# Packed attention into a softplus FFN: scores issued beside the products of M, one run for both groups' packed values, and written queues for VectorE and ScalarE

## The chip, the cores and the metric

The kernel runs on one core of a Trainium2 chip. The metric is the device time in microseconds of one execution; three executions are known. A profile of one execution gives the engines' rows.

## What is computed

```python
q, k, v: (8, 8, 576, 64)   p: (8, 8, 32, 64)   w_in: (512, 2048)   w_out: (2048, 512)   float32
packed = softmax(scale * p @ k.T) @ v          # 32 packed values per head
att    = softmax(scale * q @ packed.T) @ packed
x      = att, heads side by side               # (8 * 576, 512)
h      = x @ w_in
out    = (max(h, 0) + log1p(exp(-abs(h)))) @ w_out
```

## The kernel before

A batch has 8 heads in G = 2 groups of 4 (HG). The second attention's product with the packed values is never made on its own: with M = packed @ w_in for each head, h is (attention weights) @ M, so that a batch needs M (`make_m`, float32, 64 rows by 32 columns of the array, 16 matmul records for each 512 columns of M) and then `gemm1`. Weights and M are split into a high and a low float32r part; each product is three matmuls.

The main loop runs over 128 **units**, one for each batch b and each of 16 column blocks f of the hidden layer. In a unit TensorE (PE) does, in this order: `gemm1` (L551: 12 matmuls of 288 columns, six for each half c of the 576 rows, into the two banks `ph` of the pool `ps_h`), then for t = 0 to 3 `gemm2_tile` of the unit two before (L594: three matmuls of 512 columns each), and every fourth unit (f = 2, 6, 10, 14) the products of M for two units on. The softplus of a half c is on ScalarE (ACT) `Abs` (L576), `Exp` (L577), `Ln` (L578) and on VectorE (DVE) the last step that reads the bank `ph` (L581, `SCALAR_TENSOR_TENSOR`, called STT here); then DVE makes `gh` (L566) and `gl` (L567), which PE needs two units later. The bank `ph` of a half is free when its STT is done.

The attention of batch b+1 is a generator of which the loop takes a step now and then, so that its work falls between the `gemm2_tile` calls of batch b: four visits to the scores on PE (`scores1` and `scores2`, L291, 16 records of 288 columns, 64 rows by 32 columns), two visits to the packed values (`packed`, L346, 48 records of 64 columns), transposes of the first softmax's weights (L336, copied by ACT at L337) and of the packed values (L359). DVE transposes k and q (L274), transposes the second scores out of PSUM (L370) and does most of the second softmax: `softmax2_exp` and `softmax2_div`, the second of which is a chain of five instructions that each need the one before (sum L387, add L388, reciprocal L389, product L390, transpose L394). Scores, packed values, transposes and M's products all take their PSUM banks from the two of the pool `ps_m`. At f = 15 `weights` splits the attention weights (ACT L307, DVE L495).

Every second batch `rests` adds the 64 rows that are over from two batches: at f = 1 of an even batch, behind the stores of the batch before, eight pieces of six matmuls each (L594, `acc_m`), for each of which DVE first makes `gh_m` and `gl_m` (L566, L567).

PE's queue is written down: it issues in the order of the program. The orders of DVE and ACT are chosen by the scheduler of the language.

Of the kernel before, what the change touches and what calls it, by code (L numbers as in the profile page):

```python
# [26 lines left out]
def pack_attention_then_softplus_ffn(  # L27
# [14 lines left out]
    P = 128  # L42
# [40 lines left out]

    spare = []

    def bank(nm):
# [16 lines left out]
    def pack_transposed(bg, t):  # L103
        for o in range(0, H, HG):
            ps = bank(f"ppt_{bg}_{o}")
            for i in range(HG):
                nc.tensor.transpose(ps[:D, i * P:(i + 1) * P], t[:, o + i, :], ident)
            dst = pT[:, o:o + HG, :].rearrange("x h j -> x (h j)")
            nc.vector.tensor_copy(dst[:D], ps[:D])
            nc.scalar.copy(dst[D:], ps[:D])  # L110
# [230 lines left out]
    def packed(b, g, a1T, rs):  # L341

        ps = bank(f"psp_{b}_{g}")
        for s in range(SI):
# [18 lines left out]

    def scores2(b, g, c, qT):
        pt = res[b]["pt"][g]
        ps = scores(2, b, g, c, lambda hh: pt[:, hh * J:(hh + 1) * J], qT)
        a2 = work.tile([P, C], F32, tag="a2", name=f"a2_{b}_{g}_{c}", bufs=3)
        nc.vector.transpose(a2, ps)  # L370
# [26 lines left out]
    def attention(b):  # L397
# [211 lines left out]
    def out_tile(nm):  # L609
        return cv.tile([P, 2, DM], F32, tag="x", name=f"o_{nm}", bufs=2)  # L610
# [75 lines left out]
    gs, acc = {}, None  # L686
    units = [(b, f) for b in range(B) for f in range(NF)]
    ahead, chain, due = iter(()), iter(()), 0.0
    for u in range(len(units) + LAG):
        if u < len(units):  # L690
            b, f = units[u]
            if f == 0:
                if (b + 1) % BG == 0 and b + 1 < B:
                    pack_transposed((b + 1) // BG, pt)
                ahead = attention(b + 1) if b + 1 < B else iter(())
                due = 0.0
            chain = softplus(b, f, gemm1(b, f, res[b]), gs)
            next(chain)
            if f == NF - 1:
                if (b + 2) % BG == 0 and b + 2 < B:  # L700
                    pt = load_pack((b + 2) // BG, (nc.sync,))
                for _ in ahead:
                    pass
                if b + 1 < B:
                    weights(b + 1)
        if u >= LAG:
            b2, f2 = units[u - LAG]
            gh, gl = gs.pop((b2, f2))
            if f2 == 0:
                acc = [ps_acc.tile([P, DM], F32, tag="acc", name=f"acc_{b2}_{t}") for t in range(NT)]  # L710
        last = u >= LAG and f2 == NF - 1 and b2 % 2 == 1
        if last:
            both = rests(b2)
            next(both)
        for t in range(NT):
            if u >= LAG:
                gemm2_tile(
                    acc[t], gh, gl, f2, slice(t * P, (t + 1) * P), f2 == 0, f2 == NF - 1
                )
                if f2 == NF - 1:  # L720
                    if t % 2 == 0:
                        o = out_tile(f"{b2}_{t}")
                    store(o[:, t % 2], acc[t], [(0, b2, t * P, P)])
# [48 lines left out]
```

## Time and profile before

| | us |
|---|---|
| executions | 775.4, 775.71, 776.82 |
| median | 775.71 |
| the profiled execution | 775.68 |
| its span, first to last instruction | 773.5 |
| PE busy | 745.7 (96%) |
| DVE busy | 535.8 (69%) |
| ACT busy | 436.5 (56%) |
| mean granted clock of PE | 0.986 of 2.4 GHz |

About 2.2 us lie outside the span. In the rows below a time is from the start of the span, "us" is the duration of the instruction, and `x16` is a count of rows merged into one. Matmuls overlap in the pipeline, so that what one costs is the distance between two starts, not its duration.

### The profile page before, as it was taken

To read this page: it belongs to the slowest core of one execution; us is meant where nothing else is said; L and a number is where in the kernel's file an instruction comes from. 1 tells how busy PE (TensorE), PEld (TensorE's weight loads), DVE (VectorE), ACT (ScalarE), POOL (GpSimd) and SP (SyncE) were. 2 spreads that over 40 slices of the span, in tenths; PEclk is the share of its full clock that TensorE was granted. 3 is DMA by queue.
4 is the path that set the end of the run, shared out by engine and by line. 5 is a ranking of instruction groups with operands and counts; after the bars stand their busy time and mean duration, and the time that the engine had idled before them with its cause. 6 is when DMAs were issued, how large, how long until landed. Compare 5 with 4: busy or idle time off the path is not lost.

```text
span 773.5 us, 14441 instructions
## 1 busy us (share of the span) xinstructions
PE 745.7 (96%) x5436; PEld 589.6 (76%) x5436; DVE 535.8 (69%) x1264; ACT 436.5 (56%) x1086; POOL 92.3 (12%) x166
## 2 busy tenths in 40 slices
PE   6888998899999999999999999999999999999997
PEld 4766776677788787777788777877887777888886
DVE  2688799975787557875687567875687557765553
ACT  5668787556454555665554455565554465565540
POOL 1415443200000000000000000000000000000110
PEclk9789999999999999999999999999999999999999
DMA  9976655652322334124122233225122200010001
GB/s 229 242 166 174 171 157 138 102 107 42 62 39 70 53 62 75 32 73 76 31 48 70 45 62 59 35 66 83 32 39 78 45 1 2 0 55 1 1 1 68
DMA packets 163397, 55.97 MB, mean 72 GB/s; under 512 B 143872, under 2 KB 156672, under 8 KB 163328
## 3 DMA queue, kind: packets, MB, share of 16 engines
q1 hardware_dynamic: 162704, 54.80, 32.7%
q8 instruction: 42, 0.69, 0.4%
q10 hardware_dynamic: 624, 0.26, 0.1%
q14 instruction: 27, 0.22, 0.1%
HBM read 45.61 MB, written 9.44 MB: 71 GB/s over the span
## 4 chain that ended last, share of the span: by engine, by line
PE 84%; DVE 7%; ACT 3%; DMA 3%; issue 1%; SPq 1%; POOL 0%; DVEq 0%; ACTq 0%; POOLq 0%
PE acc L594 43%; PE ph L551 26%; PE acc_m L594 6%; PE psm L513 4%; PE ps L291 3%; PE psp L346 2%; DMA q<-in_q 2%; PE psa L336 1%; DVE t L218 1%; DMA x_i<-in_moe_w_in 1%; DVE t L213 1%; ACT m L207 1%; DVE wo_l L253 1%; DVE e L581 1%; PE psT_q L278 1%
## 5 line engine op out<-in xcount | busy, mean ns | idle before, releaser
L576 ACT ACTIVATE e<-ph 128x288 f32<-128x288 f32 x256 | 102.8, 403 | 208.5 <-PE ph L551 191.3
L581 DVE SCALAR_TENSOR_TENSOR e<-ph,e 128x288 f32<-128x288 f32 x256 | 113.8, 452 | 145.0 <-ACT e L578 144.9
L594 PE MATMUL acc<-wo_h,gh 128*128 128x512 f32 x512 | 208.0, 406 | 0.0
L594 PE MATMUL acc<-wo_l,gh 128*128 128x512 f32 x512 | 201.5, 393 | 0.0
L594 PE MATMUL acc<-wo_h,gl 128*128 128x512 f32 x512 | 201.3, 393 | 0.0
L551 PE MATMUL ph<-at_h,mh 128*128 128x288 f32 x512 | 157.7, 309 | 4.3 <-DVE e L581 4.1
L551 PE MATMUL ph<-at_l,mh 128*128 128x288 f32 x512 | 151.3, 298 | 1.3 <-DVE at_l L495 1.1
L551 PE MATMUL ph<-at_h,ml 128*128 128x288 f32 x512 | 151.6, 296 | 0.0
L551 PEld LDWEIGHTS ph<-at_h,mh 128*128 128x128 f32 x512 | 96.5, 189 | 39.8 <-DVE gl L567 16.8
L587 POOL COPY rest<-e 128x64 f32<-128x64 f32 x128 | 46.8, 366 | 581.5 <-DVE e L581 568.4
L594 PEld LDWEIGHTS acc<-wo_h,gh 128*128 128x128 f32 x512 | 96.5, 189 | 25.3 <-issue 9.8
L594 PEld LDWEIGHTS acc<-wo_h,gl 128*128 128x128 f32 x512 | 96.5, 189 | 21.5
L577 ACT ACTIVATE e<-e 128x288 f32<-128x288 f32 (+1 forms) x240 | 109.2, 455 | 3.6
L578 ACT ACTIVATE e<-e 128x288 f32<-128x288 f32 (+1 forms) x240 | 109.3, 455 | 2.9
L594 PEld LDWEIGHTS acc<-wo_l,gh 128*128 128x128 f32 x512 | 96.7, 189 | 13.2
L551 PEld LDWEIGHTS ph<-at_l,mh 128*128 128x128 f32 x512 | 96.4, 189 | 6.0 <-DVE at_l L495 3.4
L551 PEld LDWEIGHTS ph<-at_h,ml 128*128 128x128 f32 x512 | 96.7, 189 | 0.2
L567 DVE TENSOR_TENSOR gl<-e,gh 128x512 fp32r<-128x512 f32 x128 | 86.8, 678 | 4.9
L566 DVE CAST gh<-e 128x512 fp32r<-128x512 f32 x128 | 58.0, 453 | 5.6
L528 ACT CAST mh<-psm 128x512 fp32r<-128x512 f32 (+1 forms) x72 | 35.6, 543 | 40.8 <-PE psm L513 40.7
L529 DVE TENSOR_TENSOR ml<-psm,mh 128x512 fp32r<-128x512 f32 (+1 forms) x72 | 42.5, 621 | 16.9 <-ACT mh L528 16.9
L513 PE MATMUL psm<-w_in_sb,pt 64*32 64x512 f32 (+1 forms) x576 | 40.4, 561 | 4.6 <-ACT a1T L337 1.9
(79 smaller groups left out, 750.6 us busy)
## 6 DMA issues: line engine op xcount, KB each, us to landing
v<-in_v SPq DMA_DIRECT2D x16, 576.0 KB, 5.1
x_i<-in_moe_w_in SPq DMA_DIRECT2D x32, 256.0 KB, 4.8
x_o<-in_moe_w_out SPq DMA_DIRECT2D x16, 512.0 KB, 3.6
k<-in_k SPq DMA_DIRECT2D x48, 144.0 KB, 3.2
q<-in_q SPq DMA_DIRECT2D x48, 144.0 KB, 3.0
out<-o SPq DMA_DIRECT2D x24, 256.0 KB, 2.0
k<-in_k SPq DMA_DIRECT2D x4, 576.0 KB, 9.9
q<-in_q SPq DMA_DIRECT2D x4, 576.0 KB, 9.1
```

What stands on the lines that cost most here:

```text
L513: nc.tensor.matmul(ps[hh * J:(hh + 1) * J, :n], res["pt"][g][o:o + D, hh * J:(hh + 1) * J], w_in_sb[o:o + D, hh, c * n:(c + 1) * n], start ...
L528: nc.scalar.copy(mh[:, cols], ps[:, :n])
L529: nc.vector.tensor_tensor(ml[:, cols], ps[:, :n], mh[:, cols].bitcast(F32), op=ALU.subtract)
L551: nc.tensor.matmul(ph[:, :C], x[:, o:o + P], y[:, g, cs], start=(i == 0), stop=(i == 3 * G - 1),)
L566: nc.vector.tensor_copy(hi, x)
L567: nc.vector.tensor_tensor(lo, x, hi.bitcast(F32), op=ALU.subtract)
L576: nc.scalar.activation(es[c], hv[c], AF.Abs)
L577: nc.scalar.activation(e[:, x], e[:, x], AF.Exp, scale=-1.0)
L578: nc.scalar.activation(e[:, x], e[:, x], AF.Ln, bias=1.0)
L581: nc.vector.scalar_tensor_tensor(es[c], hv[c], 0.0, es[c], op0=ALU.max, op1=ALU.add)
L587: nc.gpsimd.tensor_copy(rest[:, rest_at(b, f), r:r + REST], e[:, NT * P:])
L594: nc.tensor.matmul(acc, x[:, cs], y[:, f, :], start=(first and i == 0), stop=(last and i == 2),)
```

## The change

Five edits:

- The attention of batches 2 to 7 is no longer a generator. `attention_in_slots(b)` fills a table `steps`: at unit (b-1)*16+f, slot t = 0 to 3 (behind the `gemm2_tile` of that t) or slot END = 4 (behind all four, just ahead of M's products) stands a list of calls. Batches 0 and 1 keep the generator.
- The four pairs of scores of a batch go to slot END of f = 14 (of the batch before), 2, 6 and 10, directly ahead of `make_m`, and take the two banks of `ps_h` instead of banks of `ps_m` (batch 2's first pair keeps `ps_m` and slot 0 of f = 2).
- The packed values of both groups are one run of 96 records into one bank (slot 0 of f = 5).
- From unit 16 on DVE and ACT issue in the order of the program too. For these units softplus is `Abs`, `Exp`, `Ln` of half 0, then of half 1, ahead of slot 0; the STT of half 0 is emitted behind the calls of slot 0, that of half 1 behind those of slot 2, `gh` and `gl` behind those of slot 3; stores come behind them.
- The buffers `a2` go from three to two, `pp` from one to two; the packing of p for batches 4 to 7 moves from the end of batch 2 into it.

```diff
+        def pair(nm, g):
+            return [bank(f"ps{nm}_{b}_{g}_{c}", ps_h) for c in range(2)]
...
+        def pack():
+            pp["ps"] = bank(f"psp_{b}")
+            for g in range(G):
+                pack_products(b, g, a1T[g], pp["ps"][:, g * D:])
...
+        END = NT
+        early = b == BY_BLOCK
+        for hh in range(HG):
+            if early:
+                at(hh // 2, hh % 2 * 2 + 1, move, "k", 0, hh)
+                at(2, hh, move, "k", 1, hh)
+            else:
+                at(hh // 2 - 3, hh % 2 * (1 + (hh < 2)) + (hh < 2), move, "k", 0, hh)
+                at(hh // 2 * 2, hh % 2 * (1 + (hh < 2)) + (hh < 2), move, "k", 1, hh)
+            at(3 + hh // 2, 1 + hh % 2 * 2, move, "q", 0, hh)
+            at(9 + hh // 2, hh % 2 * (1 + (hh < 2)) + (hh < 2), move, "q", 1, hh)
+        if early:
+            steps[(b - 1) * NF + 2, 0].insert(0, (score1, (0, False)))
+            n = 2
+        else:
+            at(-2, END, score1, 0)
+            n = 0
...
+        at(n, 2, exp1, 0)
...
+        at(n, 0, turn1, 0, 0)
+        at(n, 2, turn1, 0, 1)
+        at(2, END, score1, 1)
+        at(2, END, load, "q", b, 1)
+        at(4, 0, max1, 1)
+        at(4, 0, exp1, 1)
+        at(5, 0, sum1, 1)
+        at(4, END, turn1, 1, 0)
+        at(4, END, turn1, 1, 1)
+        at(5, 0, pack)
+        for g in range(G):
+            at(5, 0, load, "k", b + 1, g)
+            at(5, 1, scale_pack, g)
+            at(5, 3, turn_pack, g)
+        for g in range(G):
+            f = 6 + 4 * g
+            at(f, END, score2, g)
+            at(f, END, load, "v", b + 1, g)
+            for c in range(2):
+                at(f + 2, 2 * c, exp2, g, c)
+                at(f + 3 + c, 2 * c, div2, g, c)
...
         for x in parts:
-            for c in range(2):
-                if x.start <= c * C < x.stop:
-                    nc.scalar.activation(es[c], hv[c], AF.Abs)
+            for c in inside(x):
+                nc.scalar.activation(es[c], hv[c], AF.Abs)
             nc.scalar.activation(e[:, x], e[:, x], AF.Exp, scale=-1.0)
             nc.scalar.activation(e[:, x], e[:, x], AF.Ln, bias=1.0)
-            for c in range(2):
-                if x.start <= c * C < x.stop:
-                    nc.vector.scalar_tensor_tensor(
-                        es[c], hv[c], 0.0, es[c], op0=ALU.max, op1=ALU.add
-                    )
-        yield
+            if x.stop < S:
+                yield
+        yield
+        for x in parts:
+            for c in inside(x):
+                nc.vector.scalar_tensor_tensor(
+                    es[c], hv[c], 0.0, es[c], op0=ALU.max, op1=ALU.add
+                )
+            if x.stop < S:
+                yield
+                yield
         yield
...
+    ordered = {mybir.EngineType.DVE, mybir.EngineType.Activation}
     for u in range(len(units) + LAG):
+        if u == NF:
+            ctx.enter_context(tc.manual_schedule(engines=ordered))
...
                 if b + 1 < B:
                     weights(b + 1)
+            if b:
+                next(chain)
...
             if u < len(units):
+                for fn, args in steps.pop((u, t), ()):
+                    fn(*args)
                 due += PACE
...
             next(chain, None)
+            if u >= LAG and f2 == NF - 1:
+                if t % 2 == 0:
+                    o = out_tile(f"{b2}_{t}")
+                store(o[:, t % 2], acc[t], [(0, b2, t * P, P)])
         if last:
             next(both)
+        if u < len(units):
+            for fn, args in steps.pop((u, NT), ()):
+                fn(*args)
```

In the table of calls `move` is one transpose of k or q on DVE (L274), `turn1` three transposes on PE (L336) with their copy on ACT, `score1` and `score2` the two score halves with their copies out (ACT L307, DVE L370), `scale_pack` and `turn_pack` L354 and L359 with L361, `exp2` and `div2` are `softmax2_exp` and `softmax2_div`.

## Rows read from the trace of the kernel before

**Rows 1.** The page: busy time of each engine over the span, its share of it, and the count of its instructions.

```profile
PE 745.7 (96%) x5436; PEld 589.6 (76%) x5436; DVE 535.8 (69%) x1264; ACT 436.5 (56%) x1086; POOL 92.3 (12%) x166
```

**Rows 2.** Busy time by stretch: the units of batch 0, of batch 4 (with `rests`) and of batch 5 (without). Columns: stretch, its length, busy time and instructions of PE, PEld, DVE, ACT, POOL, then the granted clock, DMA share and GB/s.

```profile
45.10:153.80 108.70, 95.63 (x744) 71.34 (x742) 96.50 (x212) 84.00 (x179) 39.85 (x39) 0.97 0.59 148
...
410.90:503.90 93.00, 92.97 (x671) 73.79 (x670) 63.76 (x160) 47.33 (x125) 5.86 (x17) 1.00 0.28 53
503.90:585.80 81.90, 81.89 (x624) 64.91 (x623) 58.12 (x144) 47.46 (x125) 5.92 (x17) 1.00 0.29 57
```

**Rows 3.** Waits of PE within batch 0 (45.1 to 153.8 us), the longest in total: waiting line, released by; us in total, times, the longest.

```profile
PE ph L551 <- DVE e L581: 4.1, 4, 2.3
```

**Rows 4.** PE's timeline over one unit without any extra work: the first `gemm1` matmul, the first `gemm2_tile` matmul, the next unit's first. Columns: start, duration, engine, line, operation, tiles, array tile, shape, count.

```profile
489.70 0.29 PE L551 MATMUL ph<-at_h,mh 128*128 128x288 f32 x1
...
491.29 0.39 PE L594 MATMUL acc<-wo_h,gh 128*128 128x512 f32 x1
...
494.04 0.30 PE L551 MATMUL ph<-at_h,mh 128*128 128x288 f32 x1
```

**Rows 5.** PE's timeline around one visit to the scores, between two `gemm2_tile`.

```profile
444.70 0.39 PE L594 MATMUL acc<-wo_h,gl 128*128 128x512 f32 x1
445.02 0.71 PE L291 MATMUL ps<-T_k,pT 64*32 64x288 f32 x16
445.66 0.50 PE L594 MATMUL acc<-wo_h,gh 128*128 128x512 f32 x1
446.00 0.39 PE L594 MATMUL acc<-wo_l,gh 128*128 128x512 f32 x1
```

**Rows 6.** The same around one set of M's products, at the end of a unit, with the first two matmuls of the next.

```profile
457.64 0.40 PE L594 MATMUL acc<-wo_h,gl 128*128 128x512 f32 x1
457.96 1.09 PE L513 MATMUL psm<-w_in_sb,pt 64*32 64x512 f32 x16
458.98 0.40 PE L551 MATMUL ph<-at_h,mh 128*128 128x288 f32 x1
459.22 0.29 PE L551 MATMUL ph<-at_l,mh 128*128 128x288 f32 x1
```

**Rows 7.** The same around one visit to the packed values, at the end of the unit that precedes the one starting at 453.08 us.

```profile
451.95 0.40 PE L594 MATMUL acc<-wo_h,gl 128*128 128x512 f32 x1
452.27 0.88 PE L346 MATMUL psp<-v,a1T 96*32 96x64 f32 x48
453.08 0.40 PE L551 MATMUL ph<-at_h,mh 128*128 128x288 f32 x1
453.32 0.30 PE L551 MATMUL ph<-at_l,mh 128*128 128x288 f32 x1
```

**Rows 8.** ACT's timeline in the unit that starts on PE at 453.08 us: `Abs` of half 0, `Exp` of half 0, `Ln` of half 0 (half 1's `Abs` between the last two).

```profile
454.25 0.41 ACT L576 ACTIVATE e<-ph 128x288 f32<-128x288 f32 x1 [2.32 <-PE ph L551]
454.69 0.45 ACT L577 ACTIVATE e<-e 128x288 f32<-128x288 f32 x1
...
455.33 0.43 ACT L578 ACTIVATE e<-e 128x288 f32<-128x288 f32 x1
```

**Rows 9.** DVE's timeline in the same unit: the STT of half 0.

```profile
455.87 0.46 DVE L581 SCALAR_TENSOR_TENSOR e<-ph,e 128x288 f32<-128x288 f32 x1 [2.10 <-ACT e L578]
```

**Rows 10.** DVE's timeline where instructions that don't need each other follow one another: the distance of two starts is below the duration.

```profile
434.56 0.46 DVE L581 SCALAR_TENSOR_TENSOR e<-ph,e 128x288 f32<-128x288 f32 x1 [0.28 <-ACT e L578]
434.93 0.47 DVE L274 STREAM_TRANSPOSE T_k<-k 128x288 f32<-128x288 f32 x1
435.32 0.71 DVE L316 TENSOR_REDUCE m<-a 128x1 f32<-128x576 f32 x1
```

**Rows 11.** Groups by line on DVE, the four instructions of `softmax2_div` ahead of its transpose: busy us, mean ns of one, idle before.

```profile
L390 DVE TENSOR_TENSOR a<-a,z 128x288 f32<-128x288 f32 x32 | 14.4, 451 | 0.2
L387 DVE TENSOR_REDUCE z<-a 128x9 f32<-128x288 f32 x32 | 13.7, 428 | 0.2
L389 DVE RECIPROCAL z<-z 128x9 f32<-128x9 f32 x32 | 6.1, 191 | 0.3
L388 DVE TENSOR_SCALAR z<-z 128x9 f32<-128x9 f32 x32 | 6.0, 189 | 0.3
```

**Rows 12.** DVE's timeline in the unit with `rests` that starts on PE at 415.62 us: the splits of the first two pieces, two of the four stores' copies, and the split of the unit's own softplus.

```profile
416.45 0.49 DVE L566 CAST gh_m<-rest 128x256 fp32r<-128x256 f32 x2
...
419.43 1.28 DVE L618 COPY o<-acc 128x512 f32<-128x512 f32 x2
420.62 0.42 DVE L566 CAST gh<-e 128x512 fp32r<-128x512 f32 x1
...
421.56 0.68 DVE L567 TENSOR_TENSOR gl<-e,gh 128x512 fp32r<-128x512 f32 x1
```

**Rows 13.** ACT's timeline: the exponential of the first softmax with the reading of its sum.

```profile
448.48 0.78 ACT L323 ACTIVATE a<-a,nm 128x576 f32<-128x576 f32 x1 [0.33 <-DVE nm L318]
449.17 0.19 ACT L323 ACTIVATION_READ_ACCUMULATOR a<-a,nm 128x1 f32 x1
```

**Rows 14.** DVE's timeline at the end of batch 4 (the next batch's `gemm1` starts at 503.93 us): three of the four splits of the attention weights.

```profile
503.60 1.23 DVE L495 TENSOR_TENSOR at_l<-aT,at_h 128x288 fp32r<-128x288 f32 x3
```

**Rows 15.** DVE's timeline just ahead of the first unit: the transpose of group 1's first score half into `a2`, and the transpose that reads group 0's first `a2` last.

```profile
42.38 0.48 DVE L370 STREAM_TRANSPOSE a<-ps 128x288 f32<-128x288 f32 x1 [0.61 <-PE ps L291]
...
43.99 0.47 DVE L394 STREAM_TRANSPOSE aT<-a 128x288 f32<-128x288 f32 x1
```

More of the change, by code (lines that the diff above doesn't have):

```diff
@@ L84, in pack_attention_then_softplus_ffn, with bank @@
     spare = []
-    def bank(nm):
+    def bank(nm, pool=None):
+        if pool:
+            return pool.tile([P, 512], F32, tag="h", name=nm)
         if spare:
@@ L285, in transposed, with scores @@
         return dst
-    def scores(nm, b, g, c, lhs, rhs):
-        ps = bank(f"ps{nm}_{b}_{g}_{c}")
+    def scores(nm, b, g, c, lhs, rhs, ps=None):
+        if ps is None:
+            ps = bank(f"ps{nm}_{b}_{g}_{c}")
         for hh in range(HG):
@@ L307, in copy_half, with scores1 @@
         copy(half(b, c, dst), by_half(b, src))
-    def scores1(b, g, c, kT, a1):
+    def scores1(b, g, c, kT, a1, ps=None):
         cols = slice(b % BG * J, (b % BG + 1) * J)
-        ps = scores(1, b, g, c, lambda hh: pT[:, g * HG + hh, cols], kT)
-        copy_half(b, c, nc.scalar.copy, a1, ps)
+        ps = scores(1, b, g, c, lambda hh: pT[:, g * HG + hh, cols], kT, ps)
+        copy_half(b, c, nc.scalar.copy, a1, ps[:, :C])
     def softmax1_max(b, g, a1):
@@ L343, in packed, with pack_products @@
         ps = bank(f"psp_{b}_{g}")
+        pack_products(b, g, a1T, ps)
+        return pack_scaled(b, g, ps, rs)
+    def pack_products(b, g, a1T, ps):
         for s in range(SI):
@@ L351, in packed, with pack_scaled @@
                 )
-        pp = small.tile([P, 2, D], F32, tag="pp", name=f"pp_{b}_{g}", bufs=1)
+    def pack_scaled(b, g, ps, rs):
+        pp = small.tile([P, 2, D], F32, tag="pp", name=f"pp_{b}_{g}", bufs=2)
         for i in range(2):
@@ L362, in packed_transposed, with scores2 @@
         return pt
-    def scores2(b, g, c, qT):
+    def scores2(b, g, c, qT, ps=None):
         pt = res[b]["pt"][g]
-        ps = scores(2, b, g, c, lambda hh: pt[:, hh * J:(hh + 1) * J], qT)
-        a2 = work.tile([P, C], F32, tag="a2", name=f"a2_{b}_{g}_{c}", bufs=3)
-        nc.vector.transpose(a2, ps)
+        ps = scores(2, b, g, c, lambda hh: pt[:, hh * J:(hh + 1) * J], qT, ps)
+        a2 = work.tile([P, C], F32, tag="a2", name=f"a2_{b}_{g}_{c}", bufs=2)
+        nc.vector.transpose(a2, ps[:, :C])
         return a2
@@ L482, in attention, with attention_in_slots, at, move @@
         yield
+    steps = {}
+    def attention_in_slots(b):
+        kT, qT = {0: [], 1: []}, {0: [], 1: []}
+        a1, nm, rs, a1T, pp, a2 = {}, {}, {}, {}, {}, {}
+        def at(f, t, fn, *args):
+            steps.setdefault(((b - 1) * NF + f, t), []).append((fn, args))
+        def move(nm, g, hh):
+            {"k": kT, "q": qT}[nm][g].append(transposed(nm, b, g, hh))
+        def pair(nm, g):
+            return [bank(f"ps{nm}_{b}_{g}_{c}", ps_h) for c in range(2)]
+        def score1(g, merged=True):
+            a1[g] = work.tile([P, S], F32, tag="a1", name=f"a1_{b}_{g}")
+            pss = pair(1, g) if merged else (None, None)
+            for c in range(2):
+                scores1(b, g, c, kT[g], a1[g], pss[c])
+        def max1(g):
+            nm[g] = softmax1_max(b, g, a1[g])
+        def exp1(g):
+            rs[g] = softmax1_exp(b, g, a1[g], nm[g])
+        def sum1(g):
+            rs[g] = softmax1_sum(b, g, rs[g])
+        def turn1(g, c):
+            if c == 0:
+                pool, tag, bufs = (cv, "x", 2) if g else (work, "a1T", 1)
+                a1T[g] = pool.tile([NP, SI, P], F32, tag=tag, name=f"a1T_{b}_{g}", bufs=bufs)
+            a1_transposed(b, g, c, a1[g], a1T[g])
+        def pack():
+            pp["ps"] = bank(f"psp_{b}")
+            for g in range(G):
+                pack_products(b, g, a1T[g], pp["ps"][:, g * D:])
+        def scale_pack(g):
+            pp[g] = pack_scaled(b, g, pp["ps"][:, g * D:], rs[g])
+        def turn_pack(g):
+            res[b]["pt"].append(packed_transposed(b, g, pp[g]))
+        def score2(g):
+            pss = pair(2, g)
+            for c in range(2):
+                a2[g, c] = scores2(b, g, c, qT[g], pss[c])
+        def exp2(g, c):
+            softmax2_exp(b, g, c, a2[g, c])
+        def div2(g, c):
+            softmax2_div(b, g, c, a2[g, c])
+        END = NT
[15 more added lines that the diff above has]
+            n = 0
+        at(-2 if not early else 2, END, load, "q", b, 0)
+        at(n, 1 if early else 0, max1, 0)
+        at(n, 2, exp1, 0)
+        n = 3 if early else 2
+        at(n, 0, sum1, 0)
+        at(n, 0, turn1, 0, 0)
[16 more added lines that the diff above has]
+            at(f, END, load, "v", b + 1, g)
+            for c in range(2):
+                at(f + 2, 2 * c, exp2, g, c)
+                at(f + 3 + c, 2 * c, div2, g, c)
@@ L572, in softplus, with inside @@
         parts = [slice(0, S)] if b == 0 else [slice(c * C, (c + 1) * C) for c in range(2)]
+        def inside(x):
+            return [c for c in range(2) if x.start <= c * C < x.stop]
         for x in parts:
[L574 to L576 removed]
+            for c in inside(x):
+                nc.scalar.activation(es[c], hv[c], AF.Abs)
             nc.scalar.activation(e[:, x], e[:, x], AF.Exp, scale=-1.0)
             nc.scalar.activation(e[:, x], e[:, x], AF.Ln, bias=1.0)
[L579 to L584 removed]
+            if x.stop < S:
+                yield
+        yield
+        for x in parts:
[6 more added lines that the diff above has]
+                yield
         yield
@@ L688, in pack_attention_then_softplus_ffn @@
     ahead, chain, due = iter(()), iter(()), 0.0
+    for b in range(BY_BLOCK, B):
+        attention_in_slots(b)
+    ordered = {mybir.EngineType.DVE, mybir.EngineType.Activation}
     for u in range(len(units) + LAG):
+        if u == NF:
+            ctx.enter_context(tc.manual_schedule(engines=ordered))
         if u < len(units):
@@ L692, in pack_attention_then_softplus_ffn @@
             if f == 0:
-                if (b + 1) % BG == 0 and b + 1 < B:
-                    pack_transposed((b + 1) // BG, pt)
-                ahead = attention(b + 1) if b + 1 < B else iter(())
+                ahead = attention(b + 1) if b + 1 < BY_BLOCK else iter(())
                 due = 0.0
+            if (b + 2) % BG == 0 and b + 2 < B:
+                if f == 3:
+                    pt = load_pack((b + 2) // BG, (nc.sync,))
+                if f == 10:
+                    pack_transposed((b + 2) // BG, pt)
             chain = softplus(b, f, gemm1(b, f, res[b]), gs)
```

9 lines of the change are left out of this document (2 added, 7 removed).

## The prediction

> **What bounds the kernel now.** I read the page first: TensorE (PE) is busy in 96% of the span, VectorE (DVE) in 69%, ScalarE (ACT) in 56% [rows 1]. Since a busy PE may still wait, I then took the busy time by stretch: in batches 4 and 5 PE is busy in all but 0.03 us of 174.9, at the granted clock 1.00; only in batch 0 does it idle, 13 of 108.7 us [rows 2]. So from batch 1 on PE's queue is full, what is taken out of it is time won, and a wait that is put into it is time lost: nothing on PE can absorb it. The waits of batch 0 show the wait to look for, `gemm1` standing for the STT that reads a `ph` bank, 4 times, up to 2.3 us [rows 3]. Last I read PE's starts around each small group, to learn what a visit costs over its columns, and DVE's and ACT's chains in one unit, to learn when they are done.
>
> **What the change takes from PE.** A unit without extras lasts 4.34 us on PE, 1.59 for the 12 matmuls of 288 columns and 2.75 for the 12 of 512: 0.13 and 0.23 each [rows 4]. A visit to the scores: from the last `gemm2` start ahead of it, 444.70, to the second start behind it, 446.00, are 1.30 us; less two plain starts (0.46), 0.84. M's products, which have the same array tile: 457.64 to 459.22 less 0.23 and 0.13, 1.22 [rows 6]. Inside, from first start to the next line, the scores take 0.64 for 288 columns and M's products 1.02 for 512 [rows 5, 6]: 0.38 for 224 columns, so 288 columns are worth 0.48, and 0.84 - 0.48 = 0.36, say 0.35, is the price of going there and back. Set directly ahead of M's products the scores don't pay it. Six batches with four visits, less batch 2's first, which stays alone: 23 x 0.35 = 8.1 us.
>
> The packed values cost 451.95 to 453.32 less 0.23 and 0.13 = 1.01 a visit [rows 7], 0.20 of it at the two edges and the rest the run of 0.81. The trace of before has no double run. One visit less saves at least the edges, 0.20, and at most the 0.36 of the scores; I take 0.34, nearer to the scores, as the run also drains: 6 x 0.34 = 2.0. The transposes (L336, L359) are as many as before and only stand elsewhere: nothing. Won in all: 10.1 us (9.3 to 10.5).
>
> **What the written queues put in.** Times now count from the first `gemm1` matmul of a unit; without extras PE is through its 24 matmuls at 4.34 [rows 4]. `Abs` of half 0 starts at 1.06 (1.17 in the row, less 0.11 because that unit began with a tile change, its first gap being 0.24 for 0.13 [rows 7]); `Exp` 0.44 later at 1.50; `Ln` behind it (0.45 and a gap of 0.03) at 1.98, done at 2.41 [rows 8]; the STT follows 0.11 behind [rows 8, 9], at 2.52.
>
> *Units f = 10 and f = 14.* DVE's written order there is: STT of half 0, a transpose (slot 1), the whole of `div2` (slot 2), and only then the STT of half 1. Starts: STT 2.52, transpose +0.37, sum +0.39 [rows 10] = 3.28; the sum, the addition, the reciprocal and the product each need the one before, 0.43 + 0.19 + 0.19 + 0.45 [rows 11] and four gaps of 0.03, so the transpose of `div2` is at 4.66, the STT of half 1 at 5.05 and done at 5.51. Now the score pair in slot END takes the `ph` banks: its half 1 needs that STT. PE would start it at 4.34 + 0.09 = 4.43 (the first edge: 445.02 - 444.70 - 0.23) and gets it at 5.51: 1.08 us of waiting. Behind it on PE stand M's products and the next `gemm1`; before, the scores had `ps_m` banks and nobody wanted half 1's STT before 5.14 (4.34 and six matmuls). The pair is at f = 10 in six batches, and at f = 14 in five: 11 x 1.08 = 11.9. At f = 10 the copy out of half 0 (L370) also queues behind `gh` and `gl`, done at about 7.1, when PE has M's products done at 7.0: 6 x 0.1 = 0.6, as the next `gemm1` wants that bank. Bounds for the 11.9: if the small operations run at the distance of independent ones the wait is 0.7, if the semaphores take more, 1.3: 7.7 to 14.3. Units f = 2 and 6 have no `div2`: STT of half 1 is done by about 4.2, no wait.
>
> The Trainium skill bears on this place: its page TensorE: Matmul & The Clock Gate, section Part 2: What happens when you issue a matmul, says that only weight loads are pulled ahead and "The MATMULs themselves stay in program order". By that rule M's products can't step ahead of the waiting half; no row here shows a PE that could have. The rival below prices the opposite.
>
> *`rests`.* Three times, at f = 1 of an even batch. Today the scheduler puts the splits of the first two pieces together, ahead of the stores (`gh_m` x2) [rows 12]. Written down, the second piece's split comes behind four copies to the stores, both STTs and the unit's own `gh` and `gl`: STT 2.52, then two copies (0.37, 0.60), STT (0.60), copy (0.37), `gh` (0.60), `gl` (0.5), copy (0.6), `gh_m` (0.6) at 6.8, done at 7.1 [rows 10, 12]. PE has done the first piece, six matmuls of 0.23, at 4.34 + 1.38 = 5.72: 1.3 us waiting; 3 x 1.3 = 3.9 (2.4 to 4.5).
>
> *Smaller ones.* At f = 4 the first softmax's exponential is behind both halves' softplus on ACT, at about 3.6, done 0.69 + 0.19 later [rows 13] at 4.45, when PE asks for it at 4.34: 6 x 0.1 = 0.6. At f = 15 four `at_l` now stand ahead of the STT of half 0, which ends near 4.8; the next `gemm1` wants its bank at 4.34. That takes the place of a wait of like size for the `at_l` themselves, whose last ends at 504.83 with `gemm1` begun at 503.93 [rows 14]; 6 x 0.1 more = 0.6. Batch 2's prelude has the last k transpose in slot 3 of the unit whose END needs it, behind a maximum (0.71 [rows 10]) that waits for two score copies: about 1.1, once. Two `a2` buffers for three: the transpose at 42.38 must wait for the one from 43.99 to 44.46 [rows 15], 0 to 2.1 us just ahead of the first unit, where DVE has other work to fill in: 0.5. In batch 0 the STT is emitted a slot later but the scheduler still orders it: 0, within -2 to +2, as PE idles 13 us there anyway. The loads keep many units of lead, for instance k at f = 5 for use from f = 13, and M's splits are as many as before: 0, hidden in DVE's 31% of idle.
>
> **The sum**, against the profiled execution's own 775.68 (span 773.5, 2.2 outside; the median is 775.71, so it stands for the runs): 775.7 - 8.1 - 2.0 + 11.9 + 0.6 + 3.9 + 0.6 + 0.6 + 1.1 + 0.5 = 784.8, 785 in round numbers.
>
> **Rivals.**
> *DVE is in time* (other side): the STT of half 1 is done by 4.43 at f = 10 and 14, so the 11.9 and the 0.6 fall away: 772.3. It decides at the work between the two STT starts: up to 1.45 us (4.43 - 0.46 - 2.52) nothing waits, and I count 2.53. For it: DVE's starts overlap [rows 10]; against: `div2` is a chain. 0.14.
> *Every wait is covered*: only the gain stays, 765.6. PE's full queue [rows 2] speaks for a large worth of small groups, nothing for the covers. 0.04.
> *PE works on in the wait*: M's products fill 0.85 (512 columns at the 0.38 us for 224), of each 1.08: 784.8 - 11 x 0.85 = 775.4, no change. 0.06, since every row shows lines in program order.
> *The visits don't merge*: PE pays the edge between scores and M all the same: 784.8 + 8.1 = 792.9. Against it, both have one array tile, 64*32 [rows 5, 6]. 0.08.
> *Head and batch 0 worse*: the scheduler's new order there and the two `a2` cost 5 more, 790 and up: 0.06.
>
> **How the numbers follow.** The forecast, 780 to 789 by its terms' bounds, has 0.62. A change under 0.2% (1.6 us) can't be told from none by a measurement of this kernel. Slower: 0.62 + 0.08 + 0.06 = 0.76; same 0.06; faster 0.14 + 0.04 = 0.18. Predicted is the likeliest, 785. The range takes in the forecast, the third rival and most of the first (0.62 + 0.06 + 0.12) and leaves out the others: 771 to 790.
>
> **What would show it.** Right: PE's units f = 10 and f = 14 near 7.0 us with a wait of the scores for the STT of about 1 us; units f = 2 and 6 with 32 records of one tile in a row and no wait; one run of 96 records at f = 5; the second piece of `rests` waiting 1.3 us for `gh_m`. Wrong: f = 10 near 5.9, or f = 2 and 6 no shorter in sum than before's visits; a batch 0 off its 108.7 us by more than 3.

## The result, and the profile after

The changed kernel takes 786.06 us (median of 6 runs, 783.12 to 788.4) against 775.89 for the kernel before (6 runs in the same job): ratio 1.0139, 95% interval 1.0113 to 1.0165, slower by 10.2 us. Forecast were 785 and "slower", from +9.1 on the profiled execution's 775.68.

The page after, busy time by engine as in [rows 1]:

```profile
PE 745.4 (95%) x5436; PEld 595.5 (76%) x5436; DVE 552.9 (70%) x1264; ACT 464.7 (59%) x1086; POOL 91.6 (12%) x166
```

PE is as long busy as before although the small visits are cheaper, so the total tells little: batch 0 is 2.7 us longer busy, at a lower mean clock (0.94 for 0.97), the later batches less, and matmuls still in flight while PE stands for the next one count as busy. The stretches tell more; they answer to [rows 2] (batch 0, batch 4 with `rests`, batch 5 without; same columns):

```profile
44.80:155.00 110.20, 98.37 (x740) 72.88 (x740) 95.37 (x209) 84.56 (x179) 38.58 (x39) 0.94 0.62 150
...
419.70:514.70 95.00, 92.42 (x670) 74.55 (x670) 67.00 (x159) 51.40 (x125) 5.52 (x16) 1.00 0.27 52
514.70:597.30 82.60, 81.20 (x622) 65.74 (x622) 60.59 (x142) 51.47 (x125) 5.77 (x16) 1.00 0.29 57
```

Where PE had 0.03 us of idle in batches 4 and 5 it has 4.0 now, at the same granted clock of 1.00; its busy time there fell by 0.55 and 0.69. Who it waits for, in the stretch from 155 to 750 us (line, released by; us in total, times, longest):

```profile
PE ps L294 <- DVE e L699: 5.8, 11, 1.5
PE acc_m L715 <- DVE gh_m L678: 3.8, 3, 1.3
PE ph L663 <- DVE e L699: 2.0, 6, 0.4
PE ph L663 <- DVE a L379: 0.9, 5, 0.2
```

Before, no wait of PE stood in this stretch. L294 are the scores (L291 before), L699 the STT (L581 before), L715 `gemm2_tile`, L678 `gh`. The first row has the eleven waits of the forecast. Its 5.8 us are less than they cost: the row counts only time in which PE had nothing left in its pipeline. What they cost is read from the starts. PE's timeline at the end of unit f = 10 of batch 4, which began at 482.42:

```profile
486.51 0.39 PE L715 MATMUL acc<-wo_h,gl 128*128 128x512 f32 x1
486.83 0.69 PE L294 MATMUL ps<-T_q,pt 64*32 64x288 f32 x8
487.96 0.45 PE L294 MATMUL ps<-T_q,pt 64*32 64x288 f32 x4 [0.44 <-DVE e L699]
487.99 0.63 PE L625 MATMUL psm<-w_in_sb,pt 64*32 64x512 f32 x4
...
489.68 0.40 PE L663 MATMUL ph<-at_h,mh 128*128 128x288 f32 x1 [0.17 <-DVE a L379]
```

and DVE's in that unit:

```profile
484.92 0.46 DVE L699 SCALAR_TENSOR_TENSOR e<-ph,e 128x288 f32<-128x288 f32 x1 [0.80 <-ACT e L693]
485.29 0.47 DVE L276 STREAM_TRANSPOSE T_q<-q 128x288 f32<-128x288 f32 x1
485.69 0.41 DVE L396 TENSOR_REDUCE z<-a 128x9 f32<-128x288 f32 x1
486.13 0.17 DVE L397 TENSOR_SCALAR z<-z 128x9 f32<-128x9 f32 x1
486.34 0.21 DVE L398 RECIPROCAL z<-z 128x9 f32<-128x9 f32 x1
486.59 0.46 DVE L399 TENSOR_TENSOR a<-a,z 128x288 f32<-128x288 f32 x1
487.08 0.48 DVE L403 STREAM_TRANSPOSE aT<-a 128x288 f32<-128x288 f32 x1
487.49 0.42 DVE L699 SCALAR_TENSOR_TENSOR e<-ph,e 128x288 f32<-128x288 f32 x1
```

The chain of the forecast is there step by step: STT of half 0 at 2.50 us of the unit (forecast 2.52), the sum of `div2` at 3.27 (3.28), its transpose at 4.66 (4.66), the STT of half 1 at 5.07 (5.05), done at 5.49 (5.51). Half 0's scores start at 4.41 (4.43), half 1's at 5.54, where without a wait they follow 0.03 behind: 1.10 us. Each float32 matmul leaves two records here. M's first products start 0.03 behind the first four records of half 1, none before them; that far the trace agrees with the Trainium skill (TensorE: Matmul & The Clock Gate, Part 2: What happens when you issue a matmul), by which matmuls stay in program order. Half 1's second records start only at 488.23, behind those first products of M.

The gain is there too. Unit f = 6 has no `div2` in its queue, and the visit to scores and M's products is one:

```profile
467.48 0.39 PE L715 MATMUL acc<-wo_h,gl 128*128 128x512 f32 x1
467.79 0.72 PE L294 MATMUL ps<-T_q,pt 64*32 64x288 f32 x16
468.30 1.06 PE L625 MATMUL psm<-w_in_sb,pt 64*32 64x512 f32 x16
469.30 0.40 PE L663 MATMUL ph<-at_h,mh 128*128 128x288 f32 x1
469.54 0.29 PE L663 MATMUL ph<-at_l,mh 128*128 128x288 f32 x1
```

467.48 to 469.54 less the plain 0.23 and 0.13 are 1.70 us, against 0.84 + 1.22 = 2.06 for the two visits of [rows 5, 6]: 0.36 saved, as priced. So PE doesn't pay the edge between scores and M, and the rival by which the visits don't merge falls. And the packed values in one run, for [rows 7]:

```profile
459.15 0.39 PE L715 MATMUL acc<-wo_h,gl 128*128 128x512 f32 x1
459.47 1.55 PE L353 MATMUL psp<-v,a1T 96*32 96x64 f32 x96
460.95 0.50 PE L715 MATMUL acc<-wo_h,gh 128*128 128x512 f32 x1
461.28 0.40 PE L715 MATMUL acc<-wo_l,gh 128*128 128x512 f32 x1
```

459.15 to 461.28 less 0.46 are 1.67, against 2 x 1.01: 0.35 saved, 0.34 forecast.

`rests` in batch 4, PE's first piece's last matmul and the second piece's first, then DVE:

```profile
429.57 0.39 PE L715 MATMUL acc_m<-wo_h,gl_m 128*128 128x512 f32 x1
431.23 0.50 PE L715 MATMUL acc_m<-wo_h,gh_m 128*128 128x512 f32 x1 [1.27 <-DVE gh_m L678]
```

```profile
429.16 0.42 DVE L678 CAST gh<-e 128x512 fp32r<-128x512 f32 x1
429.68 0.69 DVE L679 TENSOR_TENSOR gl<-e,gh 128x512 fp32r<-128x512 f32 x1
430.29 0.68 DVE L739 COPY o<-acc 128x512 f32<-128x512 f32 x1
430.89 0.28 DVE L678 CAST gh_m<-rest 128x256 fp32r<-128x256 f32 x1
```

The second piece's split is the last of that queue, behind the unit's own split and the fourth store, where [rows 12] had it ahead of all stores; PE waits 1.27 us (forecast 1.3).

Unit lengths, each from a unit's first `gemm1` matmul to the next unit's, in batch 5 (no `rests`). Five of the kernels of the experiments stand in it beside the two:

| f | before | after | e1 | e3 | e5 | e6 | e8 |
|---|---|---|---|---|---|---|---|
| 0 | 4.72 | 4.41 | 4.41 | 5.50 | 4.41 | 4.81 | 4.85 |
| 2 | 6.32 | 6.61 | 6.61 | 6.61 | 6.61 | 6.60 | 6.61 |
| 3 | 4.47 | 4.45 | 4.45 | 4.96 | 4.45 | 4.45 | 4.45 |
| 4 | 5.45 | 5.08 | 5.08 | 5.04 | 5.08 | 4.92 | 4.92 |
| 5 | 5.69 | 6.26 | 6.29 | 6.27 | 6.26 | 6.27 | 6.27 |
| 6 | 5.90 | 6.03 | 6.04 | 6.03 | 6.03 | 6.01 | 5.53 |
| 7 | 4.90 | 4.46 | 4.46 | 4.47 | 4.46 | 4.45 | 5.99 |
| 8 | 5.37 | 4.33 | 4.33 | 4.37 | 4.33 | 4.33 | 4.44 |
| 9 | 5.08 | 4.33 | 4.33 | 4.43 | 4.33 | 4.33 | 4.33 |
| 10 | 5.69 | 7.26 | 7.52 | 5.92 | 5.92 | 5.92 | 5.44 |
| 11 | 4.45 | 4.45 | 4.44 | 4.46 | 4.47 | 4.47 | 5.97 |
| 12 | 5.21 | 4.33 | 4.33 | 4.37 | 4.33 | 4.35 | 4.41 |
| 14 | 5.45 | 7.02 | 5.92 | 5.92 | 5.92 | 5.94 | 6.11 |
| 15 | 4.44 | 4.95 | 4.95 | 4.99 | 4.95 | 4.45 | 4.44 |

(f = 1 and 13 are plain units of 4.33 to 4.44 in all.) Batch 5 as a whole: 81.8 us before, 82.6 after, 80.2 in e5, 80.0 in e6.

### The profile page after: what moved, and what is told of

Read it like the earlier page. It is cut to its first block, busy times and chain, and to the rows that moved or that the text cites. A ratio compares the mean times of both kernels' runs of the same rounds, so it can differ in the third digit from the quotient of the medians.

```text
span 785.1 us, 14466 instructions
## 1 busy us (share of the span) xinstructions
PE 745.4 (95%) x5436; PEld 595.5 (76%) x5436; DVE 552.9 (70%) x1264; ACT 464.7 (59%) x1086; POOL 91.6 (12%) x166
## 4 chain that ended last, share of the span: by engine, by line
PE 66%; DVE 9%; ACT 4%; issue 1%; DVEq 0%; ACTq 0%
PE acc L715 33%; PE ph L663 21%; PE acc_m L715 5%; PE psm L625 3%; DVE e L699 2%; PE ps L294 1%; DVE at_l L607 1%; ACT e L692 1%; ACT e L693 1%; PE psa L339 1%; PE psp L353 1%; ACT e L691 1%; DVE gl L679 1%; DVE o L739 1%; DVE aT L403 1%
## 5 line engine op out<-in xcount | busy, mean ns | idle before, releaser
L715 PE MATMUL acc<-wo_h,gh 128*128 128x512 f32 x512 | 204.2, 399 | 0.0
L715 PE MATMUL acc<-wo_l,gh 128*128 128x512 f32 x512 | 201.5, 394 | 0.0
L715 PE MATMUL acc<-wo_h,gl 128*128 128x512 f32 x512 | 201.3, 393 | 0.0
L699 DVE SCALAR_TENSOR_TENSOR e<-ph,e 128x288 f32<-128x288 f32 x256 | 114.5, 452 | 120.8 <-ACT e L693 120.8
L692 ACT ACTIVATE e<-e 128x288 f32<-128x288 f32 (+1 forms) x240 | 110.6, 461 | 7.4
L693 ACT ACTIVATE e<-e 128x288 f32<-128x288 f32 (+1 forms) x240 | 110.6, 461 | 7.2
L715 PEld LDWEIGHTS acc<-wo_h,gl 128*128 128x128 f32 x512 | 96.5, 189 | 21.0
L715 PEld LDWEIGHTS acc<-wo_h,gh 128*128 128x128 f32 x512 | 96.5, 188 | 18.0 <-issue 2.3
L715 PEld LDWEIGHTS acc<-wo_l,gh 128*128 128x128 f32 x512 | 96.6, 189 | 14.8
L679 DVE TENSOR_TENSOR gl<-e,gh 128x512 fp32r<-128x512 f32 x128 | 88.4, 691 | 8.3
L678 DVE CAST gh<-e 128x512 fp32r<-128x512 f32 x128 | 55.8, 436 | 4.9
L625 PE MATMUL psm<-w_in_sb,pt 64*32 64x512 f32 (+1 forms) x576 | 45.7, 561 | 2.4 <-DVE a L379 1.2
```

The lines of the kernel that those rows point to most:

```text
L625: nc.tensor.matmul(ps[hh * J:(hh + 1) * J, :n], res["pt"][g][o:o + D, hh * J:(hh + 1) * J], w_in_sb[o:o + D, hh, c * n:(c + 1) * n], start ...
L678: nc.vector.tensor_copy(hi, x)
L679: nc.vector.tensor_tensor(lo, x, hi.bitcast(F32), op=ALU.subtract)
L699: nc.vector.scalar_tensor_tensor(es[c], hv[c], 0.0, es[c], op0=ALU.max, op1=ALU.add)
L715: nc.tensor.matmul(acc, x[:, cs], y[:, f, :], start=(first and i == 0), stop=(last and i == 2),)
```

## The experiments

Theory A is that of the forecast: the saved visits are worth 10 us on PE, and the order in which DVE's queue is written down eats them and more, above all by `div2` and the stores in front of instructions that PE stands for. Theory B: a score pair that takes the banks of `ph` is late whatever DVE does. Theory C: the pairs in these banks lose more than they win under any order.

**e1: half 1's STT ahead of slot 2's calls.**

```diff
+                if b and t == 2:
+                    next(chain)
                 for fn, args in steps.pop((u, t), ()):
                     fn(*args)
...
-            next(chain, None)
+            if not (u < len(units) and b and t == 2):
+                next(chain, None)
```

> The changed kernel, with the STT of half 1 emitted ahead of slot 2's calls from unit 16 on, so that `div2` no longer stands before it in VectorE's queue. Theory A (the waits at f = 10 and f = 14 are half 1's STT queued behind `div2`): f = 14 falls from 7.0 us to about 6.0, the length of f = 6, because its scores are copied out by ScalarE; f = 10 stays near 7.3, because its scores are copied out by VectorE (L379) and that copy now queues behind `div2`, `gh` and `gl`, so that the next `gemm1` waits instead of the scores. In all 5 x 1.0 us less: about 781. Theory B (a score pair in the banks of `ph` waits about 1 us whatever VectorE does in that unit): f = 10 and f = 14 both stay, 786.

783.84 us, ratio 1.0124 (1.0101 to 1.0146): less than expected fell away. f = 14 went from 7.02 to 5.92, as A says; f = 10, which A left near 7.3, rose from 7.26 to 7.52, and the waits changed hands. PE's waits, 160 to 750 us:

```profile
PE ph L663 <- DVE a L379: 9.3, 6, 1.7
PE acc_m L715 <- DVE gh_m L678: 3.8, 3, 1.3
...
PE ps L294 <- DVE e L699: 0.3, 1, 0.3
```

The eleven waits for the STT are one of 0.3; at f = 10 the next `gemm1` waits in their place, six times, for the copy out of half 0 (L379). Batch 4's f = 10, which begins at 481.76 in this kernel, on DVE and then on PE:

```profile
485.44 0.46 DVE L699 SCALAR_TENSOR_TENSOR e<-ph,e 128x288 f32<-128x288 f32 x1 [0.34 <-ACT e L693]
...
488.75 0.84 DVE L379 STREAM_TRANSPOSE a<-ps 128x288 f32<-128x288 f32 x2
```

```profile
489.28 0.40 PE L663 MATMUL ph<-at_h,mh 128*128 128x288 f32 x1 [1.53 <-DVE a L379]
```

The copy stands behind `div2`, `gh` and `gl` in both kernels. It starts at 6.99 us of the unit here and at 6.73 in the changed kernel (489.15), because `div2` now stands behind an STT for which DVE itself has to wait. So at f = 10 the STT's place alone decides nothing: the length of DVE's queue up to the copy sets the unit either way. Theory B falls: the same pair in the same banks waits or doesn't by what is queued ahead of it. What was off in the expectation is f = 10, which paid more (7.52 for 7.26); in batch 2 f = 10 and 11 together grew by 2.3 us, for a reason that no run settles.

**e5: the second softmax one unit earlier**, so that f = 10 and f = 14 hold no `div2`.

```diff
-                at(f + 2, 2 * c, exp2, g, c)
-                at(f + 3 + c, 2 * c, div2, g, c)
+                at(f + 1, 2 * c, exp2, g, c)
+                at(f + 2 + c, 0, div2, g, c)
```

> The changed kernel, with the second softmax one unit earlier: `exp2` at f = 7 and 11, `div2` at slot 0 of f = 8, 9, 12 and 13, so that no `div2` is left in the units f = 10 and 14. Theory A: f = 10 falls from 7.26 to about 6.03 and f = 14 from 7.02 to about 6.03, both the length of f = 6, no other unit grows: 6 x 1.2 + 5 x 1.0 = 12.2 us less, about 774. Theory B (the pair waits whatever VectorE does): 786. A third way, that the wait moves with `div2` (f = 9 and 13 grow by about 1 us each): 784 to 786.

771.94 us, ratio 0.9977 (0.9957 to 0.9997): just below the kernel before, and by the two ratios 1.6% or 12.5 us below the changed kernel. f = 10 and f = 14 are 5.92 to 5.97 (in batch 2, which packs p, f = 10 went from 8.43 to 7.08), and no other unit from 16 on grew. PE's waits, 160 to 750 us, all of them:

```profile
PE acc_m L715 <- DVE gh_m L678: 3.8, 3, 1.3
PE ph L663 <- DVE e L699: 1.9, 6, 0.3
```

This settles the largest term: two calls in other slots, the same instructions, and the eleven waits and the copy's are gone.

**e2: the second piece of `rests` split with the first.**

```diff
+            if i != n:
                 split(gh[:, cs], gl[:, cs], rest[:, o:o + n, :].rearrange("x f j -> x (f j)"))
             if i == 0:
+                o = rest_at(b, fs[n])
+                c2 = slice(n * P, 2 * n * P)
+                split(gh[:, c2], gl[:, c2], rest[:, o:o + n, :].rearrange("x f j -> x (f j)"))
                 yield
```

> The changed kernel, with the split of the second piece of `rests` emitted directly behind that of the first, ahead of the stores. Theory A (PE waits for `gh_m` because the written order puts it behind four copies to the stores, both STTs and the unit's own split): the three units with `rests` fall from 16.8 us to about 15.5, the wait of L715 for L678 goes, 3.7 us less in all: about 782. Rival (the two STTs and stores, now later, hold something else up): the units stay near 16.8 or the next one grows, 786.

783.02 us, ratio 1.0124 (1.0094 to 1.0153); by the medians alone the 3.0 us below 786.06 can't be told from the runs' spread (the ratio went from 1.0139 only to 1.0124), but by the units they can: with `rests` they go from 16.79, 16.77 and 16.77 to 15.54, 15.58 and 15.61, and the wait for `gh_m` is in no row of that kernel.

**e3: the scheduler's queues again**, all else as changed.

```diff
-        if u == NF:
-            ctx.enter_context(tc.manual_schedule(engines=ordered))
```

> The changed kernel without the written queues of VectorE and ScalarE: the scheduler orders them again, everything else is as changed (score pairs in the banks of `ph` beside M's products, one run of packed values). Theory A (the loss lies in the written order alone): the waits at f = 10, f = 14 and in `rests` go or shrink, the gain of 10 us on PE stays: 766 to 775, below the kernel before. Rival C (the score pairs in the banks of `ph` lose more than the saved visits give, under any order of the other engines): 780 or more.

779.93 us, ratio 1.0074 (1.0053 to 1.0095): between the two expectations and above A's. The waits that A names did go (f = 10 and f = 14 are 5.92, in batch 2 6.38, the units with `rests` 15.53), so the loss of these units isn't the pairs' own; that C falls as a whole only e6 shows, which is below the kernel before with all pairs in these banks. Others came, 0.5 us at f = 3, 1.1 at f = 0 and, once, 2.1 at f = 6 of batch 1. ACT's timeline in the unit f = 15 of batch 4, which began at 506.24:

```profile
508.12 0.78 ACT L326 ACTIVATE a<-a,nm 128x576 f32<-128x576 f32 x1 [0.70 <-DVE nm L321]
508.81 0.18 ACT L326 ACTIVATION_READ_ACCUMULATOR a<-a,nm 128x1 f32 x1
508.90 0.39 ACT L691 ACTIVATE e<-ph 128x288 f32<-128x288 f32 x1
```

The scheduler puts the first softmax's exponential in front of `Abs`, and ACT stands for its maximum until 508.12; `Abs` starts at 2.66 us of the unit instead of 1.06, and all behind it is late. So "the loss lies in the written order alone" is wrong as a sentence about this program: its calls are emitted in an order that the scheduler, too, turns into waits, 7.8 us of them for the STT from 160 to 750 us. With the same calls the scheduler's queues are 6 us better than the written ones (779.93 against 786.06), and e5's calls in written queues are 8 us better still. No run has e5's calls with the scheduler's queues, so that the queues had to be written is not shown.

**e4: the head as before** (three `a2` buffers, with one `pp` buffer making room, and batch 0's STT behind its activations).

```diff
-        a2 = work.tile([P, C], F32, tag="a2", name=f"a2_{b}_{g}_{c}", bufs=2)
+        a2 = work.tile([P, C], F32, tag="a2", name=f"a2_{b}_{g}_{c}", bufs=3)
...
-            if b:
-                next(chain)
+            next(chain)
```

> The changed kernel, with what the change does ahead of unit 16 undone: three `a2` buffers again (room for them from one `pp` buffer that takes turns with the tag x) and in batch 0 the STT emitted directly behind the activations. Theory A (batch 0 and the head lost 1.3 us by these two, the rest of the loss lies behind unit 16): units 0 and 1 of batch 0 fall from 11.3 and 6.2 to about 10.2 and 4.7, the units from 16 on stay, 784 to 785. Rival (the two `a2` buffers also hold up the batches behind): units behind 16 shrink too, 782 or less.

785.83 us, ratio 1.0140 (1.0109 to 1.0172): no difference that can be measured. In its one profile units 0 and 1 fell from 11.27 and 6.16 to 10.31 and 4.67 us, but f = 5 of batch 0 rose from 5.70 to 6.86; batch 0 as a whole was 1.25 shorter, and the units from 16 on stayed. That the two edits cost batch 0 its 1.3 us doesn't follow: in e1 and e5, which keep both and touch nothing ahead of unit 16, batch 0 came out 1.3 shorter as well. Two things are mixed. Unit 0 takes 11.3 to 11.7 us in the five kernels with both edits (the changed one, e1, e2, e3, e5) and 9.6 to 10.3 in the six without. Unit 1 goes with TensorE's granted clock, in the changed kernel and in e5 (columns as in [rows 2]):

```profile
56.08:62.25 6.17, 4.19 (x20) 3.90 (x19) 3.45 (x9) 5.34 (x12) 1.69 (x3) 0.67 0.45 99
```

```profile
56.01:60.66 4.65, 2.36 (x18) 2.17 (x19) 3.45 (x9) 4.65 (x11) 1.50 (x2) 1.00 0.42 108
```

DVE and ACT issue in the same order in both up to unit 16. In the changed kernel the clock is at its lower level, 1.2 of 2.4 GHz, from 53.3 to 60.1 us, in e5 from 50.5 to 53.9, within unit 0; in both PE had stood for up to 1.7 us for `at_h` in that unit.

**e6: every named wait taken away**: e5, e2 and e4 together, the packing of p in f = 11, `max1` and `exp1` of group 1 in f = 3, and at f = 15 half 0's STT ahead of the `at_l`.

```diff
-        at(4, 0, max1, 1)
-        at(4, 0, exp1, 1)
+        at(3, 0, max1, 1)
+        at(3, 3, exp1, 1)
...
             if x.stop < S:
+                if f == NF - 1:
+                    last_step(x)
                 yield
...
-                if f == 10:
+                if f == 11:
                     pack_transposed((b + 2) // BG, pt)
```

> The changed kernel with every named wait taken away: the second softmax one unit earlier, the second piece of `rests` split with the first, the packing of p in f = 11, the first softmax's second exponential in f = 3, half 0's STT ahead of the four `at_l` at f = 15, and the head as in the kernel before. Theory A (the saved visits are worth 10 us on PE and only these waits ate them): against the 771.9 of the shift alone 3.7 for `rests`, 1.2 for p, 0.6 for f = 4, 1 to 1.5 for f = 15, 0 to 1.5 for the head: 763 to 767, 8 to 11 us below the kernel before. Rival (with these waits gone others come up in their place): 768 or more.

766.8 us (6 runs), ratio 0.9908 (0.9876 to 0.9940): below both kernels. Two of its parts did not do what they should. At f = 15 and f = 0 the wait mostly moved, from half 0's bank to half 1's (4.95 and 4.41 became 4.45 and 4.81). The packing of p, ahead of `gemm1` of f = 11, waits for the banks that M's splits still read, and batch 2's f = 10 stayed at 8.38:

```profile
PE ph L664 <- DVE e L692: 1.4, 6, 0.3
PE ppt L109 <- DVE ml L642: 1.4, 1, 1.4
```

(PE's waits, 160 to 760 us, all of them.)

**e9: p packed in slot 3 of f = 11**, on top of e6.

```diff
-                    pack_transposed((b + 2) // BG, pt)
+                    steps.setdefault((u, 3), []).append((pack_transposed, ((b + 2) // BG, pt)))
```

> The mended kernel, with the packing of p (eight transposes on PE, two copies on VectorE, two on ScalarE behind them) in slot 3 of f = 11 of batch 2 instead of ahead of that unit's `gemm1`. Theory A (ahead of `gemm1` the packing's copies stand in front of the unit's softplus in the written queue of ScalarE, and at f = 11 its banks wait for M's splits; behind both it is covered): in batch 2, f = 10 falls from 8.4 to 5.9 us and f = 11 grows by its transposes, 0.8 us; 1.6 us less than the mended kernel from the first unit to the last, one place, and about 8 to 9 us less than the kernel before in the median. Rival (the packing costs the same wherever it stands): the sum of f = 10 to 13 stays.

765.57 us (4 runs), ratio 0.9876 (0.9831 to 0.9922), the lowest median of all, though not to be told from e6's by the times. Batch 2's f = 10 is 5.96, f = 11 5.23, the batch 1.41 us shorter than in e6; what is left of PE's waits behind 160 us is 1.4 us, all at f = 0.

**e7: two runs of packed values**, on top of e6.

```diff
-        at(5, 0, pack)
         for g in range(G):
+            at(5, g, pack, g)
```

(with `scale_pack` a slot later.)

> The mended kernel, with the packed values of the two groups as two runs again (behind the first and the second `gemm2_tile` of f = 5). The one-run edit was priced at 0.34 us a batch between bounds of 0.20 and 0.36: unit f = 5 grows from about 6.26 by 0.2 to 0.36 us, 1.2 to 2.2 us in all. If the run itself has no drain to save, 0.20.

One run, 771.95 us, which as a total can't be told from e6's 765.65 to 773.06; f = 5 is 6.60 for 6.27 in each of six batches: 0.33, so 2.0 us in all, as forecast.

**e8: the second scores where no products of M follow**, on top of e6.

```diff
-            f = 6 + 4 * g
+            f = 7 + 4 * g
```

> The mended kernel, with the second scores (and the second softmax behind them) one unit later, in slot END of f = 7 and 11, where no products of M follow. Theory A: each of the two pairs pays its own visit again, 0.36 us, and more than that: M's products no longer stand between the pair and the next `gemm1`, so that `gemm1` waits for the copy out of half 0 (L379), which is behind `gh` and `gl` in VectorE's queue and done near 5.8 us of the unit, with PE through at 5.2: about 0.6 more. Units f = 6 and 7 together grow by 0.9 to 1.1, f = 10 and 11 likewise, 11 to 13 us in all; f = 14 may wait 0.2 for an STT behind `div2`. Rival (only the visit counts): 0.36 for each pair, 4.3 us in all.

One run, 779.87 us. f = 6 and 7 together are 11.52 for 10.46, f = 10 and 11 together 11.41 for 10.39: 1.06 and 1.02 a pair, A's 0.9 to 1.1, not the 0.36 of the visit alone. PE's waits, 160 to 750 us:

```profile
PE ph L664 <- DVE a L380: 9.0, 12, 1.0
```

Twelve waits, one for each pair, for the copy out of half 0. So to stand beside M's products is worth two things: the visit (0.36), and cover for the copy, as M's 1.0 us of PE work leaves DVE time to empty the borrowed banks (the other 0.7).

## Why the prediction was right

- *PE is the bound and can't absorb a wait.* Right: the waits are found again in the lengths of their units, and e5 gave back 12.5 us by moving work that PE doesn't do.
- *The gain, 8.1 and 2.0.* Right: 0.36 a visit and 0.35 a run by the starts, 0.33 a run by e7. By the units it is somewhat larger: without f = 15 and 0, batch 5 is 1.94 us shorter in e6 than before, where the forecast has 4 x 0.35 + 0.34 = 1.74. No run says where the other 0.2 come from.
- *f = 10 and f = 14, 11 x 1.08.* Right: 1.10 by the starts, 1.10 by f = 14 (7.02 against 5.92 in e1 and e5). The copy out of half 0 was sized 0.1 and is 0.24 (7.26 - 5.92 - 1.10). At f = 10 the sum's split into these two terms holds for the size alone: e1 took the first wait away and the second grew by more.
- *`rests`, 3 x 1.3.* Right: 1.20 by e2's units, 1.27 by the row.
- *f = 4, 6 x 0.1.* Right in place; 0.16 by e6 (3.6 + 0.69 + 0.19 of the working are 4.48, not 4.45). *f = 0, 6 x 0.1 more.* f = 15 and f = 0 together are 9.36 for 9.16: 0.2.
- *Batch 2's prelude, 1.1.* Right: f = 2 and 3 of batch 1 are 13.00 for 11.06 in the later batches, less 0.84 for the visit alone, 1.10. The wait has no row among the waits; the starts show it. PE at the end of f = 2 of batch 1, and DVE's last transpose of k:

```profile
169.15 0.40 PE L715 MATMUL acc<-wo_h,gl 128*128 128x512 f32 x1
169.48 1.55 PE L294 MATMUL ps<-T_k,pT 64*32 64x288 f32 x11
...
172.29 0.29 PE L663 MATMUL ph<-at_l,mh 128*128 128x288 f32 x1
```

```profile
170.05 0.46 DVE L276 STREAM_TRANSPOSE T_k<-k 128x288 f32<-128x288 f32 x1
```

  169.15 to 172.29 less 0.36 are 2.78 us, against the 1.70 of f = 6 above: 1.08.
- *Head and batch 0, 0.5 and 0.* Batch 0 grew by 1.56 in the profile (of 2.6 in units 0 and 1, 1.4 came back at f = 5). "The scheduler still orders it: 0" left out the clock: 1.5 of it are unit 1 at a mean of 0.67, and with that unit at 1.00, in e1 and e5, batch 0 is 108.90 and 108.97, 0.3 more than before. The bound of 2 held. Why the clock falls at another place in e5 than in the changed kernel stays open. The head's 0.5 can't be read from profiles whose first `gemm1` lies 7 us apart.
- *What was left out.* The packing of p was named in the change and not priced. Its new place, ahead of `gemm1` of f = 10 in batch 2, cost 1.2 us more than the old: that unit is 8.43 where the other batches have 7.26. ACT's timeline there (the unit before ends on PE at 303.57):

```profile
304.72 1.18 ACT L112 COPY pT<-ppt 64x512 f32<-64x512 f32 x2 [2.60 <-DVE pT L111]
305.92 0.41 ACT L691 ACTIVATE e<-ph 128x288 f32<-128x288 f32 x1
```

In the written queue ACT's two copies stand ahead of `Abs`, and they wait for DVE's, so that `Abs` starts at 2.35 us of the unit instead of 1.06 and the scores' wait is 1.5 there by the row and 2.3 by the starts (308.08 to 310.43). e9 took it away.

The mechanism was right, and the total partly by luck. Behind unit 16 the two profiles differ by 10.3 us, where the forecast has 8.6 (9.1 less the head's 0.5). Terms missed or too small there (p 1.2, the copy 0.8, f = 0 0.6, f = 4 0.4) add up to 3.0 us, and a gain 1.2 us larger than forecast made up for part of them. With batch 0's 1.56, nearly all of it the clock, the stretch from the first `gemm1` matmul to the last matmul grew by 11.9 us (723.2 to 735.1); the medians differ by 10.2, and single runs of one kernel by up to 7.4. That spread is also far above the 0.2% that the prediction held to be measurable. The stated range, 771 to 790, took in "no change" and a faster kernel, so the time alone doesn't bear out the forecast: the unit lengths, e1 and e5 do.

## What to carry to other kernels

On an engine that is the bound, a saved tile change of 0.36 us is worth as much as it is only while no wait comes in its place: before one moves a step into the banks of another, list what the releasing engine has queued in front of the release, with its starts, and compare the time with that at which the bound engine comes by. When a queue is written down, every instruction that the bound engine stands for counts: to put one of them in front of a chain of dependent small ones mended f = 14 and not f = 10, where a second one stood behind the chain. Moving the chain to a unit where nothing behind it is awaited mended both; two calls in other slots were worth 12 us. The same held for the second piece's split and p's copies. Beside a group that needs other banks a borrowed bank has time to be emptied: adjacency is worth the tile change and the cover.

## What the runs showed that was not expected

- The wait rows understate such a wait: 5.8 us in 11 rows, when the starts say 10 x 1.10 and 2.3 for batch 2's f = 10, 13.3 in all, as PE still has half 0's matmuls in the pipeline when it begins to stand. In batch 4 half 0's last record ends at 487.52, so that only 0.44 of the 1.10 us count as idle.
- Two copies out of one PSUM tile, on two engines and into different partitions, ran one behind the other (ACT's L112 waits for DVE's L111 above), as they do in the kernel before. Why is not shown.
- The head varies from run to run: e6 and e9 are the same ahead of unit 16, yet PE stood 8.6 us for the first q in e6's profile and 2.2 in e9's, and the first `gemm1` matmul lies at 50.4 and at 43.4 us. The unit lengths of one place agree within some 0.03 us from profile to profile where nothing was changed, so they tell differences of 0.1 us, while the medians hardly tell 2. The head is a part of that spread; how large a part is not shown:

```profile
PE psT_q L280 <- DMA q<-in_q: 8.6, 1, 8.6
```

```profile
PE psT_q L280 <- DMA q<-in_q: 2.2, 1, 2.2
```
